# Attention between the second products: bundles of three and four slots by group of heads, instead of bundles of three across groups

## The chip, the cores and the metric

The kernel runs on one core of a Trainium2 chip. The metric is the device time of one execution in microseconds (us). An execution is also recorded by the hardware profiler; its span, its engines' busy times and its waits are what the readings below rest on.

## The reference

For q, k and v of shape (8, 12, 448, 64), that is 8 batches, 12 heads, 448 positions and 64 per head, the reference computes an attention with a squared relu, and then a layer norm with a feed-forward block on the 768 values of each position:

```python
scores = scale * np.matmul(q, k.transpose(0, 1, 3, 2))
attn = np.maximum(scores, 0.0) ** 2 / S
attn_out = np.matmul(attn, v)
x = attn_out.transpose(0, 2, 1, 3).reshape(B, S, H * D)
xn = (x - mu) / np.sqrt(var + 1e-06) * g_ln
out = x + np.maximum(xn @ w_ch1, 0.0) @ w_ch2      # w_ch1: 768 x 3072, w_ch2: 3072 x 768
```

Inputs and output are float32; the kernel multiplies in bfloat16 and sums in float32.

## The kernel before, in words

The kernel writes out the order of its work by hand: each engine executes its instructions in the order in which the Python code issues them. What one engine must wait for on another is left to semaphores.

Batches are taken in four pairs. For a pair, the positions of both batches (896, which are 7 blocks of 128 rows, `NT`) pass the feed-forward block together. Its first product (`ffn1`, L585, and for the later pairs also `ffn1_pair`, L663) gives hT. Its second product (`ffn2`, L627) is cut into units: 7 blocks, 2 halves of the 768 columns, 4 parts each, 56 units for a pair, and a unit is 6 matmuls into a PSUM tile `o_ps` (L634). After the fourth part of a half, VectorE evicts o_ps (`finish`, L645) and SP's queue stores the rows. `o_ps` comes from the pool ps_mm, which has two tiles.

While TensorE does the second products of one pair, it also does the attention of the next pair (`attention`, L522). There are three such stages in the kernel. The 12 heads of a batch are taken in 3 groups of four, so a pair of batches has 6 groups (`lo` to `hi`), and the keys of a group are cut into J = 7 slots. One slot is `scores(n, (i,), FULL)` (L327): four matmuls of 64 rows by 64 columns by 448 that use the four quarters of the array (L335), into a tile sc_ps of the pool ps_sc; ScalarE's relu (L346) takes it from PSUM into a tile attn_sb; VectorE squares that in place (L348). When all seven slots of a group are done, `values(n, FULL)` (L354) multiplies them with v: 28 matmuls (L365) into a tile av_ps, also of ps_sc; VectorE scales it into xT (L372) and makes xc of it (L388); GpSimd adds it to a running sum of the chunks (`chunks_summed`, L392). After the third group of a batch these sums are put on TensorE with a matrix of ones, and VectorE takes the mean out of xc (`centre`, L410).

ps_sc has three tiles, used in turn (`bufs=3`, L91): a slot, a product with v and the centring sum of an even batch each take the next one and wait until what last used it has been read. attn_sb has nine tiles.

`attention` returns a list of units, and `interleave` (L13) spreads them evenly between the units of the second product: after each of those it issues as many attention units as are due. So a list with fewer units leaves more second-product units between two of them. An attention unit is a *bundle* of slots, with a product with v in it where one is due:

```python
def item(n, i):
    scores(n, (i,), FULL)
    if i == J - 1 and n + 3 < len(groups):
        transposed(n + 3)

def product(n):
    values(n, FULL)
    load(n + 4, "v")
```

After a group's last slot, `transposed(n + 3)` issues the loads of k and q on GpSimd's queue and three transposing DMAs on SP's queue (L282, L287, L288) for a later group. The list ends with the product of the last group and with the second batch's `centre`.

Before, the 42 slots of a stage are cut into 14 bundles of three, across the bounds of groups. The product of group n - 1 stands behind the last of slots 1 and 2 of group n that is among the first two of a bundle: behind slot 2 as the first of its bundle (groups 1 and 4), behind slot 2 as the second of its bundle (groups 2 and 5), or behind slot 1 as the second (group 3). The first batch's `centre` is placed two bundles behind the bundle with its last product.

Of the kernel before, what the change touches and what calls it, by code (L numbers as in the profile page):

```python
# [28 lines left out]
def kernel(  # L29
# [32 lines left out]
    J = S // HP  # L62
# [55 lines left out]
    def load(n, names):  # L118
        if n >= len(groups):
            return  # L120
        b, m = groups[n]
        for name in names:
            if b == 1 and name != "v":
                o = (2 * m + "qk".index(name)) * 2 * S
                t = hold[:, o:o + 2 * S].rearrange("p (r s) -> p r s", r=2)
            elif name == "q":
                t = qbuf[m][:, D:D + 2 * S].rearrange("p (r s) -> p r s", r=2)
            else:
                t = io.tile([P, 2, S], bf16, tag=name, name=name + "_sb", bufs=4 if name == "v" else 3)
            nc.gpsimd.dma_start(t, srcs[name][b][:, m:NP:G, :])  # L130
            qkv[name, b, m] = t
# [27 lines left out]
    for queue, name, lo, hi in ((nc.sync, "q", 0, FEW), (nc.scalar, "k", 0, FEW),  # L159
                                (nc.sync, "k", FEW, J), (nc.scalar, "q", FEW, J)):  # L160
        s = slice(lo * D, hi * D)
# [165 lines left out]
    def scores(n, slots, blk):  # L327
        g, w = st[groups[n]], blk[1] * HP
        ps = ps_sc.tile([P, 2, 512], fp32, tag="sc", name="sc_ps")
        for o, i in enumerate(slots):  # L330
            for r in range(2):
                rows = slice(r * HP, (r + 1) * HP)
                for hh in range(2):
                    cols = slice(hh * HP, (hh + 1) * HP)
                    nc.tensor.matmul(  # L335
                        ps[cols, r, o * w:(o + 1) * w], g["k"](i)[rows, cols],
                        g["q"](i, r)[rows, blk[0]:sum(blk), cols], start=True, stop=True)
        if groups[n][0]:
            a = apool.tile([P, 2, 512], bf16, tag="attn", name="attn_sb")
        else:  # L340
            o = n_early[0] % 12 * 1024
            a = early[:, o:o + 1024].rearrange("p (r s) -> p r s", r=2)
            n_early[0] += 1
        since[0] = 0
        a = a[:, :, :len(slots) * w]
        nc.scalar.activation(a, ps[:, :, :len(slots) * w], ACTF.Relu)  # L346
        if blk == FULL:
            nc.vector.tensor_mul(a, a, a)  # L348
        else:
            later.append((n, a))  # L350
        for o, i in enumerate(slots):
            g["attn"].append(a[:, :, o * w:(o + 1) * w])

    def values(n, blk):  # L354
        squares_now(n)
        b, m = groups[n]
        v_sb, g, w = qkv["v", b, m], st[groups[n]], blk[1] * HP
        ps = ps_sc.tile([P, 2, 512], fp32, tag="sc", name="av_ps")
        for j in range(J):
            for hh in range(2):  # L360
                rows = slice(hh * HP, (hh + 1) * HP)
                for pr in range(2):
                    cols = slice(pr * HP, (pr + 1) * HP)
                    i, r = g["where"](pr, j)
                    nc.tensor.matmul(  # L365
                        ps[cols, hh, :w], v_sb[rows, pr, j * D:(j + 1) * D],
                        g["attn"][i][rows, r, :], start=(j == 0), stop=(j == J - 1))
        if b // 2 not in xT:
            xT[b // 2] = xpool.tile([P, K1, S2], bf16, tag="xT", name="xT_sb")
        if b not in xc:  # L370
            xc[b] = xcpool.tile([P, K1, S], bf16, tag="xc", name="xc_sb")
        nc.vector.tensor_scalar_mul(  # L372
            xT[b // 2][:, 2 * m:2 * m + 2, of(blk, b)], ps[:, :, :w], score_scale)
        if (b, blk) != FIRST:
            scaled(b, m, blk)
        g["attn"] = []
        since[0] = 9
        if blk == FULL:
            chunks_summed(b, m)
# [30 lines left out]
    def centre(b, blk):  # L410
        w = blk[1] * HP
        straight = (b, blk) == FIRST or blk == FULL and b % 2
        if straight:
            ps = ps_mm.tile([P, 512], fp32, tag="mm", name="sum_ps")[:, :w]
        else:
            ps = ps_sc.tile([P, 2, 512], fp32, tag="sc", name="sum_ps")[:, 0, :w]
        rows = [xT[b // 2][:, c, of(blk, b)] for c in range(K1)]
        if blk == FULL:
            rows = [part[b][:, i] for i in range(2)] + (rows[4:] if b % 2 else [])
        for i, r in enumerate(rows):  # L420
            nc.tensor.matmul(ps, ones, r, start=(i == 0), stop=(i == len(rows) - 1))  # L421
        total = ps
        if not straight:
            total = spool.tile([P, S], fp32, tag="total", name="total_sb", bufs=1)[:, :w]
            nc.scalar.copy(total, ps)
        for c in range(K1):
            nc.vector.scalar_tensor_tensor(
                xc[b][:, c, of(blk)], total, g_mean[:, c:c + 1], xc[b][:, c, of(blk)],
                op0=ALU.mult, op1=ALU.add)
# [3 lines left out]
    def transposed(n):  # L433

        if groups[n][0] < by_dma:
            transposes(*groups[n])
            return


        if n > by_dma * G:  # L440
            load(n + 2, "kq")
        keys_dma(n)
        queries_dma(n)

    def attention_block(b, blk):


        lo, hi, first = b * G, b * G + G, blk[0] == 0
        units = [lambda: transposed(lo)] if first else []

        def unit(n, part):
            squares_now()
            for i in range(4 * part, min(4 * part + 4, J), 2):
                scores(n, tuple(range(i, min(i + 2, J))), blk)
            if b == 1 and not first and part and n == hi - 1:
                transposed(hi)
            if part and n > lo:
                values(n - 1, blk)
                if not first:
                    load(n + 3, "v")  # L460
        for n in range(lo, hi):
            units.append(lambda n=n: unit(n, 0))
            if first and n + 1 < hi:
                units.append(lambda n=n: transposed(n + 1))
            units.append(lambda n=n: unit(n, 1))

        def last():
            values(hi - 1, blk)
            if b == 1 and not first:
                load(hi + 3, "v")  # L470
        units.append(last)
        units.append(lambda: centre(b, blk))
        return units
# [48 lines left out]
    def attention(bs):  # L522

        lo, hi = bs[0] * G, (bs[-1] + 1) * G
        seq = [(n, i) for n in range(lo, hi) for i in range(J)]  # L530
# [10 lines that stand above are left out]
        def bundle(items, at):  # L541
            for o, it in enumerate(items):
                item(*it)
                if o == at:
                    product(it[0] - 1)
        units, due = [], [[], []]
        for s in range(0, len(seq), 3):
            items = seq[s:s + 3]
            at = max((o for o, (n, i) in enumerate(items[:2]) if n > lo and i in (1, 2)), default=-1)
            units.append(lambda items=items, at=at: bundle(items, at))  # L550
            n = items[at][0] - 1
            due.append([groups[n][0]] if at >= 0 and groups[n][1] == G - 1 else [])
            units += [lambda b=b: centre(b, FULL) for b in due.pop(0)]
        units.append(lambda: product(hi - 1))
        units.append(lambda: centre(bs[-1], FULL))
        return units
# [428 lines left out]
    def ffn1_units(b, blk=FULL):  # L985
        if blk == FULL:
            return [lambda ni=ni: ffn1(b, ni, blk, b % 2 == 0) for ni in range(K2)]
        return [lambda: ffn1_head(b, blk)] + [lambda ni=ni: ffn1(b, ni, blk) for ni in range(3, K2)]

    def late_rows(n):  # L990

        last = [n // 2 - 1, n - 1]
        return [ki for ki in range(n) if ki not in last] + last
# [31 lines left out]
    units, side = ffn1_units(0, BLK[0][0]), attention_block(0, BLK[0][1])  # L1025
    units, late = units[:-4], units[-4:]
# [13 lines left out]
    units = ffn1_units(0, BLK[0][1])  # L1040
# [9 lines left out]
    for pair in range(pairs - 1):  # L1050
        units = ffn2_units(pair)
        if pair:
# [12 lines left out]
            units = units[2:]  # L1065
# [15 lines left out]
    def between(n):  # L1081
        for _ in range(4):
            gps.pop(0)()
        if n > 1 and side:
# [7 lines left out]
    units = [lambda half=half, part=part: ffn2(pair, 3, half, part, rows=late_rows(K2))  # L1092
             for half in range(2) for part in range(4)]
# [47 lines left out]
```

## Time and profile before

| what | value |
|---|---|
| median of 3 runs | 526.93 us (526.73 to 527.14) |
| the profiled execution's own time | 527.49 us |
| its span | 525.7 us |
| TensorE (PE) busy | 516.9 us, 98% of the span |
| VectorE (DVE) busy | 388.5 us, 74% |
| ScalarE (ACT) busy | 284.1 us, 54% |
| GpSimd (POOL) busy | 197.3 us, 38% |
| mean granted clock of TensorE | 1.00 |

The span runs from the first to the last instruction that the profiler recorded. In lines of the trace, PE is TensorE's matmuls and PEld its weight loads, which overlap; L335 is line 335 of the kernel; "x12" is a count, "128x896 bf16<-128x896 f32" the shapes written and read, and "64\*64" the part of the array that a matmul uses. What stands in brackets at the end of a line is how long the engine had been idle before it and whose instruction ended that idle time. In a list of waits the numbers are total us, how many times, and the longest.

### The profile page before, as it was taken

How to read it: one execution, taken by the hardware profiler on the slowest of the kernel's cores; microseconds unless marked ns; L12 is line 12 of the kernel's file. 1: busy time of each engine (PE TensorE's matmuls, PEld its weight loads, DVE VectorE, ACT ScalarE, POOL GpSimd, SP SyncE). 2: the span in 40 equal slices, each digit the busy share in tenths (PEclk: the TensorE clock that was granted, in tenths of full speed). 3: DMA queues.
4: the chain of work that ended last, by engine and by line, in shares of the span. 5: the costliest groups of instructions: out<-in, count | busy, mean ns of one | idle time of the engine just before them, and what ended most of it. 6: DMA issues, size and time to landing. Idle time of an engine off the chain costs nothing.

```text
span 525.7 us, 11571 instructions
## 1 busy us (share of the span) xinstructions
PE 516.9 (98%) x4612; PEld 305.5 (58%) x4612; DVE 388.5 (74%) x727; ACT 284.1 (54%) x478; POOL 197.3 (38%) x246
## 2 busy tenths in 40 slices
PE   8899999999999999999999999999999999999996
PEld 6678778755555555555555555555555554555663
DVE  5775654278898788758889779856989856886773
ACT  6966775465545266746646256647555435761110
POOL 7335102114624376002343727300330319991331
PEclk9999999999999999999999999999999999999999
DMA  9999999999988930216999885614651147421123
GB/s 196 206 206 207 211 192 164 172 159 139 171 137 153 185 68 0 36 31 102 169 170 179 134 206 172 157 36 62 131 104 46 46 111 185 116 88 31 38 54 91
DMA packets 121224, 66.50 MB, mean 126 GB/s; under 512 B 79698, under 2 KB 119890, under 8 KB 121170
## 3 DMA queue, kind: packets, MB, share of 16 engines
q1 hardware_dynamic: 92178, 37.05, 36.2%
q0 software_dynamic: 26976, 25.50, 33.0%
q10 hardware_dynamic: 2016, 3.21, 1.7%
q8 instruction: 36, 0.59, 0.5%
q14 instruction: 18, 0.15, 0.1%
HBM read 56.82 MB, written 15.93 MB: 138 GB/s over the span
## 4 chain that ended last, share of the span: by engine, by line
PE 93%; DMA 3%; POOL 2%; ACT 1%; DVE 1%; issue 0%; ACTq 0%; DVEq 0%; POOLq 0%
PE o_ps L634 34%; PE m_ps L752 21%; PE h_ps L596 15%; PE m_ps L885 8%; PE sc_ps L335 7%; PE av_ps L365 6%; DMA w<-in_moe_w_ch_dram 2%; PE h_ps L618 1%; DMA w_soon<-kept 1%; PE sum_ps L421 1%; ACT early L346 1%; PE tr_ps L220 1%; POOL v_sb L130 0%; POOL w L148 0%; POOL k_sb L130 0%
## 5 line engine op out<-in xcount | busy, mean ns | idle before, releaser
L634 PE MATMUL o_ps<-w,hT_sb 128*128 128x384 bf16 x1056 | 181.6, 326 | 0.0
L346 ACT ACTIVATE attn_sb<-sc_ps 128x896 bf16<-128x896 f32 (+4 forms) x150 | 126.4, 902 | 82.3 <-PE sc_ps L335 69.5
L634 PEld LDWEIGHTS <-hT_sb 128*128 128x128 bf16 x1056 | 99.6, 98 | 78.1 <-issue 15.2
L348 DVE TENSOR_TENSOR attn_sb<-attn_sb 128x896 bf16<-128x896 bf16 x126 | 81.6, 662 | 31.5 <-ACT attn_sb L346 26.9
L756 ACT ACTIVATE hT_sb<-m_ps 128x448 bf16<-128x448 f32 x120 | 65.2, 544 | 37.7 <-PE m_ps L752 35.7
L596 PE MATMUL h_ps<-xc_sb,w 128*128 128x192 bf16 (+2 forms) x648 | 82.2, 280 | 0.7 <-DMA w<-in_moe_w_ch_dram 0.3
L596 PEld LDWEIGHTS <-w 128*128 128x128 bf16 x648 | 58.1, 98 | 20.9 <-issue 3.1
L604 ACT ACTIVATE hT_sb<-h_ps 128x192 bf16<-128x192 f32 (+2 forms) x93 | 37.7, 406 | 56.8 <-PE h_ps L596 56.3
L400 POOL TENSOR_TENSOR part_sb<-xT_sb 128x448 f32<-128x448 bf16 x6 | 6.6, 1103 | 104.6 <-DVE xT_sb L372 84.9
L403 POOL TENSOR_TENSOR part_sb<-part_sb,xT_sb 128x448 f32<-128x448 f32 x18 | 23.3, 1295 | 55.6 <-DVE xT_sb L372 54.9
L846 POOL TENSOR_TENSOR w_sum_t<-w 128x384 bf16<-128x384 bf16 x48 | 41.8, 910 | 0.0
L752 PE MATMUL m_ps<-x_sum,w 128*128 128x448 bf16 x180 | 38.9, 352 | 0.0
L752 PE MATMUL m_ps<-xc_sb,w_sum 128*128 128x448 bf16 x168 | 36.4, 352 | 0.0
L572 DVE BATCH_NORM_STATS2 stats<-xtok_sb 128x6 f32<-128x384 bf16 x56 | 28.3, 546 | 10.7 <-DMA xtok_sb<-xT_sb 10.7
L335 PE MATMUL sc_ps<-qT_sb,kT_sb 64*64 64x448 bf16 x504 | 35.0, 358 | 0.0
L372 DVE TENSOR_SCALAR xT_sb<-av_ps 128x896 bf16<-128x896 f32 (+2 forms) x30 | 27.0, 901 | 7.8 <-PE av_ps L365 7.7
L365 PE MATMUL av_ps<-attn_sb,v_sb 64*64 64x448 bf16 (+2 forms) x672 | 32.3, 327 | 0.0
L752 PEld LDWEIGHTS <-w_sum 128*128 128x128 bf16 x210 | 20.5, 98 | 19.3 <-issue 0.3
L645 DVE SCALAR_TENSOR_TENSOR o_sb<-o_ps,rstd_sb,xtok_sb 128x384 f32<-128x384 f32 x44 | 26.6, 604 | 4.4 <-PE o_ps L634 4.4
L365 PEld LDWEIGHTS <-v_sb 64*64 64x64 bf16 x840 | 22.7, 107 | 11.8 <-issue 1.6
L388 DVE TENSOR_SCALAR xc_sb<-xT_sb,g_sb 128x448 bf16<-128x448 bf16 (+2 forms) x54 | 26.6, 541 | 1.0
L752 PEld LDWEIGHTS <-w 128*128 128x128 bf16 x180 | 17.6, 98 | 16.4
(144 smaller groups left out, 652.2 us busy)
## 6 DMA issues: line engine op xcount, KB each, us to landing
out_dram<-o_sb SPq DMA_DIRECT2D x90, 96.0 KB, 2.5
v_sb<-in_v_dram POOLq DMA_DIRECT2D x24, 224.0 KB, 5.3
w<-in_moe_w_ch_dram POOLq DMA_DIRECT2D x12, 384.0 KB, 13.9
w<-in_moe_w_ch_dram POOLq DMA_DIRECT2D x4, 1152.0 KB, 20.2
q_sb<-in_q_dram POOLq DMA_DIRECT2D x20, 224.0 KB, 6.6
k_sb<-in_k_dram POOLq DMA_DIRECT2D x20, 224.0 KB, 5.8
w_soon<-kept ACTq DMA_DIRECT2D x8, 288.0 KB, 3.5
w_late<-kept SPq DMA_DIRECT2D x10, 192.0 KB, 3.2
```

Of the source, the lines that this page charges most:

```text
L335: nc.tensor.matmul(ps[cols, r, o * w:(o + 1) * w], g["k"](i)[rows, cols], g["q"](i, r)[rows, blk[0]:sum(blk), cols], start=True, stop=True)
L346: nc.scalar.activation(a, ps[:, :, :len(slots) * w], ACTF.Relu)
L348: nc.vector.tensor_mul(a, a, a)
L365: nc.tensor.matmul(ps[cols, hh, :w], v_sb[rows, pr, j * D:(j + 1) * D], g["attn"][i][rows, r, :], start=(j == 0), stop=(j == J - 1))
L572: nc.vector.bn_stats(stats[:, n], xtok[pair][:, n * G:(n + 1) * G, t, :])
L596: nc.tensor.matmul(ps[:, :w], w1[:, c, ni * P:(ni + 1) * P], xc[b][:, c, of(blk)], start=(c == 0), stop=(c == K1 - 1))
L604: nc.scalar.activation(hT[pair][:, ni, o:o + w], ps[:, :w], ACTF.Relu)
L634: nc.tensor.matmul(ps[:, :DH], hT[pair][:, ki, t * P:(t + 1) * P], w2[:, ki, cols], start=(o == 0), stop=(o == K2 - 1))
L752: nc.tensor.matmul(ps, *at, start=(first and c == 0), stop=(c == KQ - 1), skip_group_check=not first)
L756: nc.scalar.activation(hT[pair][:, rows[n][row], half * S:(half + 1) * S], ps, ACTF.Relu)
L846: op(w2_sum[name][:, i:i + n], b[x][:, i:i + n], b[y][:, i:i + n])
L885: nc.tensor.matmul(ps, x[:, ki], y[:, ki], start=(first and ki == 0), stop=(ki == KH - 1), skip_group_check=not first)
```

## The change

The bundles are now cut by group: slots 0, 1, 2 in one bundle and slots 3, 4, 5, 6 in the next, 12 bundles a stage instead of 14. The product of group n - 1 always stands behind slot 0 of group n, as the second thing in the bundle of three. The first batch's `centre` follows one bundle behind the bundle with its last product instead of two. No instruction is added or removed: each engine executes the same ones in another order.

```diff
-        units, due = [], [[], []]
-        for s in range(0, len(seq), 3):
-            items = seq[s:s + 3]
-            at = max((o for o, (n, i) in enumerate(items[:2]) if n > lo and i in (1, 2)), default=-1)
+        units, due = [], [[]]
+        cuts = [n * J + i for n in range(hi - lo) for i in (0, 3)] + [len(seq)]
+        for s, e in zip(cuts, cuts[1:]):
+            items = seq[s:e]
+            at = max((o for o, (n, i) in enumerate(items[:1]) if n > lo and i == 0), default=-1)
             units.append(lambda items=items, at=at: bundle(items, at))
             n = items[at][0] - 1
             due.append([groups[n][0]] if at >= 0 and groups[n][1] == G - 1 else [])
             units += [lambda b=b: centre(b, FULL) for b in due.pop(0)]
```

Between two attention units of a stage there are now three or four second-product units (18 or 24 matmuls), as before, with four more often.

## The prediction

> **What bounds the kernel now.** I read the page first, for the engine that sets the end, then TensorE's own waits, then the order of work in one second-product stage, first TensorE alone and then all engines.
>
> The page:
>
> ```profile
> span 525.7 us, 11571 instructions
> PE 516.9 (98%) x4612; PEld 305.5 (58%) x4612; DVE 388.5 (74%) x727; ACT 284.1 (54%) x478; POOL 197.3 (38%) x246
> PE 93%; DMA 3%; POOL 2%; ACT 1%; DVE 1%; issue 0%; ACTq 0%; DVEq 0%; POOLq 0%
> ```
>
> TensorE is busy 98% of the span and carries 93% of the chain that ended last. So only what lengthens or shortens TensorE's own sequence moves the end. Its waits are short:
>
> ```profile
> PE idle_ps L206 <- DVE ones L99: 1.1, 1, 1.1
> PE av_ps L365 <- DMA v_sb<-in_v_dram: 0.7, 1, 0.7
> PE sc_ps L335 <- DVE early L223: 0.6, 2, 0.5
> ```
>
> These are the three longest of nine. None lies in the three stages that the change touches: by the busy times by stretch, TensorE is busy 75.20 of 75.20 us (99.8 to 175.0), 76.15 of 76.15 (222.9 to 299.0) and 76.20 of 76.20 (347.1 to 423.3). The stages run back to back:
>
> ```profile
> 111.92 3.10 PE L634 MATMUL o_ps<-w,hT_sb 128*128 128x384 bf16 x18
> 114.95 0.38 PE L335 MATMUL sc_ps<-qT_sb,kT_sb 64*64 64x448 bf16 x4
> 115.17 1.49 PE L365 MATMUL av_ps<-attn_sb,v_sb 64*64 64x448 bf16 x28
> 116.49 0.62 PE L335 MATMUL sc_ps<-qT_sb,kT_sb 64*64 64x448 bf16 x8
> 117.04 4.07 PE L634 MATMUL o_ps<-w,hT_sb 128*128 128x384 bf16 x24
> 121.04 0.76 PE L335 MATMUL sc_ps<-qT_sb,kT_sb 64*64 64x448 bf16 x12
> 121.74 3.10 PE L634 MATMUL o_ps<-w,hT_sb 128*128 128x384 bf16 x18
> 124.77 0.57 PE L335 MATMUL sc_ps<-qT_sb,kT_sb 64*64 64x448 bf16 x8
> 125.17 1.49 PE L365 MATMUL av_ps<-attn_sb,v_sb 64*64 64x448 bf16 x28
> ```
>
> The columns are start and duration. Four L335 matmuls are one slot, 28 L365 matmuls one product with v, six L634 matmuls one unit of the second product. Durations overlap at their ends, so I count from start to start. Last, the engines behind TensorE:
>
> ```profile
> 115.76 0.92 ACT L346 ACTIVATE attn_sb<-sc_ps 128x896 bf16<-128x896 f32 x1 [1.56 <-PE av_ps L365]
> 121.48 2.54 ACT L346 ACTIVATE attn_sb<-sc_ps 128x896 bf16<-128x896 f32 x3 [2.67 <-PE sc_ps L335]
> 122.43 0.63 DVE L348 TENSOR_TENSOR attn_sb<-attn_sb 128x896 bf16<-128x896 bf16 x1 [1.04 <-ACT attn_sb L346]
> 124.05 0.63 DVE L348 TENSOR_TENSOR attn_sb<-attn_sb 128x896 bf16<-128x896 bf16 x1 [0.18 <-ACT attn_sb L346]
> ```
>
> A slot takes TensorE 0.19 us; its relu takes ScalarE 0.92 us alone and 0.81 from one to the next (three in 2.54). The relu is what frees the slot's tile in ps_sc, and ps_sc has three tiles. A bundle of three slots just fits.
>
> **Fewer bundles: the part that is gained.** Six L634 matmuls take (4.00 - 3.03) = 0.97 us (24 from 117.04 to 121.04, 18 from 121.74 to 124.77), so 18 take 2.91. The 18 from 121.74 ended 3.03 later, so going to 64*64 costs 0.12. Three slots took 0.70 from 121.04 to 121.74, where three times 0.19 is 0.56, so going back costs 0.14. A bundle thus costs 0.26 beside its work. Two fewer in each of three stages: 6 x 0.26 = -1.6 us. The Trainium skill (TensorEngine Tiling, Key Properties) says that changing the tiling mode drains TensorE; by that rule alone the change would be this gain and nothing else, about 526.93 - 1.6 = 525.3 us. The trace agrees that a switch costs something, 0.12 and 0.14 us.
>
> **The fourth slot: the part that is lost.** The second bundle of each group holds slots 3 to 6: four ps_sc tiles in a row with no product between. The fourth goes into the first one's tile, and waits for its relu. From the bundle at 121.04: the first relu starts at 121.48, 0.44 after the first matmul, and lasts 0.92, so it ends 1.36 after. How long TensorE takes to go on is seen once in the lines above. In the bundle at 114.95 four tiles are asked for too (slot, product, slot, slot). Its first relu ended at 115.76 + 0.92 = 116.68; the last slot was ready at 116.49 + 0.19 = 116.68; its eight matmuls last 0.62, against 0.57 for the eight at 124.77. So TensorE goes on 0.05 after the relu's end, 1.41 after the bundle's start. Without a wait the fourth slot would start at 0.40 (two slots, 124.77 to 125.17) + 0.19 = 0.59. The wait is 0.82 us. Queued behind it on TensorE are the fourth slot and all second-product units after it, so nothing covers it. There are 6 such bundles in each of 3 stages: 18 x 0.82 = +14.8 us. Against the drain rule stands another of the Trainium skill (TensorEngine Tiling, PSUM Bottleneck): tiling speeds up TensorE but not the emptying of PSUM, which may then set the pace. The trace agrees, 0.19 us a slot against 0.81, and the sum goes by the measured rows.
>
> The bounds of this wait: if the tile came free at the relus' pitch of 0.81 and without the 0.05, it would be 0.44 + 0.81 - 0.59 = 0.66, or +11.9. If the first relu began as late as that at 115.76, 0.81 after its slot, it would be 1.19, or +21.4. I take 0.82, since the late one waited for a product that reads an attn_sb tile nine slots back, and the new order issues that product before every slot that needs it. ScalarE is also idle when a bundle begins (2.67 us before 121.48).
>
> **The product's place.** Where the product went behind the first slot of its bundle (groups 1 and 4, twice a stage), the third slot lost the 0.05 above: 6 x 0.05 = -0.3. In the new first bundles the first relu should start 0.44 after its slot and end at 1.36 + 0.05, while the third slot is reached at 0.22 + 1.32 + 0.19 = 1.73, so no wait. The product now follows the group's last slot sooner. In a bundle of four the relus start at 0.44, 1.25, 2.06 and 2.87, the last ends at 3.79, and its square at 4.45. TensorE leaves the bundle at 4 x 0.19 + 0.82 + 0.14 = 1.71, does 18 matmuls and a switch (3.03) and one slot (0.21), and begins the product at 4.95. It reads the last slot only in its sixth of seven steps, 0.95 later. Cover 1.4 us; if statistics (1.01 + 0.21) and an eviction (0.61) lay ahead on VectorE, 0.4 us would show in such a bundle.
>
> **Four squares on VectorE, and what is queued behind.** An o_ps eviction behind them starts at 4.5 instead of 3.7 us after the bundle and ends by 5.1, or 6.3 with statistics. The half that needs its bank starts after another 24 matmuls (3.88) and mostly a bundle with its product (2.0), at 1.71 + 0.97 + 5.9 = 8.6. Nothing.
>
> **The centring sum one bundle earlier.** It needs GpSimd's sums, done 6.7 us after the product's end (135.26):
>
> ```profile
> 137.51 2.67 POOL L403 TENSOR_TENSOR part_sb<-part_sb,xT_sb 128x448 f32<-128x448 f32 x2 [3.86 <-DVE xT_sb L372]
> 140.88 1.04 POOL L407 TENSOR_TENSOR two_sb<-part_sb,two_sb 128x448 bf16<-128x448 f32 x1
> 146.91 0.54 PE L421 MATMUL sum_ps<-two_sb,ones 128*128 128x448 bf16 x2
> ```
>
> Before, 5.0 us were to spare. In the new order the sum comes 0.51 (two slots) + 4.00 (24 matmuls) + 1.71 + 2.91 = 9.1 us after the product: 2.4 to spare. Were that cover gone by as much again, three sums would cost at most 7.
>
> **Loads, transposes, stores.** GpSimd's queue keeps its order, load(n+4, "v") behind the product included. On SP's queue the transposes of group n+3 stand among other output stores, which wait for evictions; they are needed two to three groups later, some 25 us. Nothing on TensorE.
>
> **Sum.** -1.6 + 14.8 - 0.3 = +12.9 us. The profiled execution took 527.49 us (span 525.7 and 1.8 around it), 0.56 above the median of 526.93. So 540.4 on its scale and **539.8 us** as a median.
>
> **Rivals.**
>
> *No wait at the fourth slot, and the switches win.* The time is 526.93 - 1.9 = 525.0. It decides where the wait is under 1.9 / 18 = 0.11 us a bundle, that is where TensorE may go on 0.59 + 0.11 = 0.70 us after the bundle's start. For it: TensorE shows no wait there today, and the queue has its work ready. Against it: the relu would have to take 0.70 - 0.44 - 0.05 = 0.21 us where the row has 0.92. This is also the case of a change that does not do what I read. Chance 0.04.
>
> *The first relu is late as well.* If ScalarE or VectorE falls behind in the closer order (VectorE is busy 58.8 of the first stage's 75.2 us), the wait goes towards 1.19 and the product and evictions wait too: +19.5, or 546.4. Against it: the waits themselves give VectorE 14.8 us more room. Chance 0.07.
>
> *The tile comes free early.* With 0.66 a bundle: +10.0, or 536.9. Chance 0.06.
>
> *The clock falls.* If after each wait the burst of 18 matmuls ran at half the granted clock, 18 x 2.91 = 52 us more, near 592. Against it: from 12 to 16 us TensorE was busy only 2.88 of 4.00 us and the granted clock in that window stayed 1.00. The Trainium skill (TensorE: Matmul & The Clock Gate, A second HAM failure mode) says that short idles between groups of matmuls, from cycling PSUM banks, can make the clock oscillate; no wait in this trace shows it. Chance 0.01.
>
> **Numbers.** The forecast, a wait near 0.82 in each of 18 bundles, has 0.82. The range 536.5 to 544.5 takes in the early tile, the forecast with half a microsecond a group lost on the late side (18 x 0.25 = 4.5), and leaves out the rest. It leaves out 0.12. Slower by over 0.2% (about what a measurement of this kernel can tell from no change) has 0.94: all cases but the one without a wait, less 0.02 for a wait so early (near 0.11 us) that it just cancels the gain, which is the same. Faster has 0.04.
>
> **What would show it.** Right: TensorE's list of waits gains an L335 line on ACT attn_sb L346 with 18 of about 0.8 us each, about 15 in all; the page's TensorE share falls to about 95%; a bundle of four lasts about 1.7 us to the next L634 matmul; each stage grows by about 4.3 us. The ScalarE wait on av_ps L365 (12.8 us in 6) goes away. Wrong: L335 shows no such wait or one under 0.3 us; or waits appear at L634 on VectorE, at L365 on the squares, or at L421 on GpSimd; or the granted clock falls under 1.00.

## The result: 2.6% slower, and the profile after

| | before | changed |
|---|---|---|
| median | 526.93 us (526.73 to 527.14, 5 runs) | 540.38 us (540.15 to 541.18, 5 runs) |
| profiled execution, its span | 527.49, 525.7 us | 540.83, 539.1 us |
| ratio | 1 | 1.0258 (95% interval 1.0243 to 1.0273) |

The change adds one line, so L634 is now L635; L335, L346, L365, L372 and L421 keep their numbers.

The page, its span, the engines and the chain that ended last:

```profile
span 539.1 us, 11569 instructions
PE 518.7 (96%) x4612; PEld 307.9 (57%) x4612; DVE 394.8 (73%) x727; ACT 283.3 (53%) x478; POOL 197.2 (37%) x246
PE 89%; DMA 5%; ACT 3%; POOL 1%; issue 1%; DVE 0%; POOLq 0%
```

Every engine in the second line has as many instructions as before, TensorE its 4612 matmuls; the two fewer in the first line are of none of them. TensorE's share falls from 98 to 96%, and ScalarE's share of the chain rises from 1 to 3%. TensorE's own waits, longest first, have a new first line:

```profile
PE sc_ps L335 <- ACT attn_sb L346: 11.5, 18, 0.6
```

There are 18 waits of scores for a relu, one for each bundle of four. The order of work on TensorE and ScalarE shows where they stand. These lines are from the first stage; columns are start and duration, and the bracket is the idle time before:

```profile
108.38 0.76 PE L335 MATMUL sc_ps<-qT_sb,kT_sb 64*64 64x448 bf16 x12
108.81 3.35 ACT L346 ACTIVATE attn_sb<-sc_ps 128x896 bf16<-128x896 f32 x4 [1.99 <-PE sc_ps L335]
109.78 0.38 PE L335 MATMUL sc_ps<-qT_sb,kT_sb 64*64 64x448 bf16 x4 [0.64 <-ACT attn_sb L346]
110.10 3.10 PE L635 MATMUL o_ps<-w,hT_sb 128*128 128x384 bf16 x18
113.12 0.38 PE L335 MATMUL sc_ps<-qT_sb,kT_sb 64*64 64x448 bf16 x4
...
113.56 0.92 ACT L346 ACTIVATE attn_sb<-sc_ps 128x896 bf16<-128x896 f32 x1 [1.40 <-PE sc_ps L335]
114.66 0.55 PE L335 MATMUL sc_ps<-qT_sb,kT_sb 64*64 64x448 bf16 x8
```

Three slots start at 108.38. ScalarE begins their relus at 108.81, idle until then. The fourth slot starts at 109.78, 1.40 us after the bundle's start, where 0.59 would do without a wait. So the wait is 0.81 us from start to start. The bracket says 0.64, because it counts from the modelled end of the matmul before, and that end lies about 0.17 us past the point where the next one could start. 18 x 0.81 = 14.6 us.

The first stage by stretch, for the changed kernel (the first number behind the bounds is its length, the second TensorE's busy time):

```profile
99.70:179.30 79.60, 75.76 (x680) 41.64 (x679) 60.40 (x106) 37.93 (x51) 28.79 (x34) 1.00 0.97 150
```

TensorE was idle 79.60 - 75.76 = 3.84 us, six times 0.64; before it was not idle at all in this stage. The other two stages read the same, 3.85 and 3.84 us. The granted clock (the number after the five engines) is 1.00 in all three. Counted in the trace from the first matmul of the unbroken second products of a stage to the first one of the next first product, the stages last 79.6, 77.7 and 77.7 us instead of 75.2, 73.3 and 73.3: 4.4 us longer each, 13.2 of the 13.4 us by which the span grew.

### The profile page after: what moved, and what is told of

It reads as the page before. It is cut to its first block, busy times and chain, and to the rows that moved or that the text cites. A ratio compares the mean times of both kernels' runs of the same rounds, so it can differ in the third digit from the quotient of the medians.

```text
span 539.1 us, 11569 instructions
## 1 busy us (share of the span) xinstructions
PE 518.7 (96%) x4612; PEld 307.9 (57%) x4612; DVE 394.8 (73%) x727; ACT 283.3 (53%) x478; POOL 197.2 (37%) x246
## 4 chain that ended last, share of the span: by engine, by line
PE 89%; DMA 5%; ACT 3%; POOL 1%; issue 1%; DVE 0%; POOLq 0%
PE o_ps L635 33%; PE m_ps L753 21%; PE h_ps L597 14%; PE m_ps L886 8%; PE sc_ps L335 6%; PE av_ps L365 6%; ACT attn_sb L346 3%; DMA w<-in_moe_w_ch_dram 3%; DMA v_sb<-in_v_dram 2%; PE h_ps L619 1%; DMA w_soon<-kept 1%; PE sum_ps L421 1%; PE tr_ps L220 1%; POOL k_sb L130 0%; POOL v_sb L130 0%
## 5 line engine op out<-in xcount | busy, mean ns | idle before, releaser
L635 PE MATMUL o_ps<-w,hT_sb 128*128 128x384 bf16 x1056 | 180.5, 327 | 0.0
L346 ACT ACTIVATE attn_sb<-sc_ps 128x896 bf16<-128x896 f32 (+4 forms) x150 | 125.9, 905 | 92.1 <-PE sc_ps L335 90.7
L635 PEld LDWEIGHTS <-hT_sb 128*128 128x128 bf16 x1056 | 100.1, 98 | 74.9 <-issue 11.1
L348 DVE TENSOR_TENSOR attn_sb<-attn_sb 128x896 bf16<-128x896 bf16 x126 | 86.6, 703 | 33.2 <-ACT attn_sb L346 30.3
L597 PEld LDWEIGHTS <-w 128*128 128x128 bf16 x648 | 58.1, 97 | 20.7 <-issue 2.9
L335 PE MATMUL sc_ps<-qT_sb,kT_sb 64*64 64x448 bf16 x504 | 36.9, 359 | 11.5 <-ACT attn_sb L346 11.5
L372 DVE TENSOR_SCALAR xT_sb<-av_ps 128x896 bf16<-128x896 f32 (+2 forms) x30 | 27.0, 901 | 9.2 <-PE av_ps L365 9.0
L335 PEld LDWEIGHTS <-kT_sb 64*64 64x64 bf16 x504 | 14.6, 105 | 32.5 <-issue 27.5
L365 PE MATMUL av_ps<-attn_sb,v_sb 64*64 64x448 bf16 (+2 forms) x672 | 32.3, 327 | 0.0
L753 PEld LDWEIGHTS <-w_sum 128*128 128x128 bf16 x210 | 20.5, 98 | 19.1
L365 PEld LDWEIGHTS <-v_sb 64*64 64x64 bf16 x840 | 22.8, 107 | 11.1 <-issue 1.6
```

What stands on the lines that cost most here:

```text
L335: nc.tensor.matmul(ps[cols, r, o * w:(o + 1) * w], g["k"](i)[rows, cols], g["q"](i, r)[rows, blk[0]:sum(blk), cols], start=True, stop=True)
L365: nc.tensor.matmul(ps[cols, hh, :w], v_sb[rows, pr, j * D:(j + 1) * D], g["attn"][i][rows, r, :], start=(j == 0), stop=(j == J - 1))
L597: nc.tensor.matmul(ps[:, :w], w1[:, c, ni * P:(ni + 1) * P], xc[b][:, c, of(blk)], start=(c == 0), stop=(c == K1 - 1))
L635: nc.tensor.matmul(ps[:, :DH], hT[pair][:, ki, t * P:(t + 1) * P], w2[:, ki, cols], start=(o == 0), stop=(o == K2 - 1))
L753: nc.tensor.matmul(ps, *at, start=(first and c == 0), stop=(c == KQ - 1), skip_group_check=not first)
```

## The experiments

The theory is that the fourth slot's wait for a tile of ps_sc is the whole loss, that two fewer bundles a stage are the whole gain, and that nothing else matters. Rivals are the product's new place with the earlier centring sum, and a backlog on ScalarE or VectorE from four slots in a row, whatever tile they free. The edits are against the changed kernel.

| kernel | median, us | before on the same chip | ratio (95% interval) | expected, us |
|---|---|---|---|---|
| 3, 2, 2 slots | 531.35 | 526.97 | 1.0097 (1.0065 to 1.0129) | 529.7 |
| 4, 3 slots, product behind slot 0 | 546.98 | 526.97 | 1.0377 (1.0360 to 1.0394) | 544.6 |
| 4, 3 slots, product behind slot 1 | 532.80 | 526.97 | 1.0114 (1.0099 to 1.0129) | 532.2 |
| first relu in two halves | 549.41 | 526.97 | 1.0436 (1.0401 to 1.0470) | 533.7 to 536.4 |
| first relu of one half only | 533.64 | 526.86 | 1.0128 (1.0111 to 1.0145) | 533.5 |
| 3, 2, 2 slots, centring sum later | 529.75 | 526.86 | 1.0051 (1.0036 to 1.0066) | 529.7 |
| 2, 2, 2, 1 slots | 534.35 | 526.86 | 1.0140 (1.0125 to 1.0155) | 534.4 |
| 13 bundles | 533.75 | 526.86 | 1.0128 (1.0113 to 1.0143) | 525.9 to 529.6 |
| four slots in three tiles | 525.60 | 527.21 | 0.9972 (0.9961 to 0.9983) | 525.2 |

**No bundle of four: 3, 2 and 2 slots.**

```diff
-        cuts = [n * J + i for n in range(hi - lo) for i in (0, 3)] + [len(seq)]
+        cuts = [n * J + i for n in range(hi - lo) for i in (0, 3, 5)] + [len(seq)]
```

> The changed kernel with slots 3 to 6 cut once more: bundles of 3, 2 and 2 slots, 18 a stage. The product stays behind slot 0 and the first batch's centre one bundle behind its last product. Theory (the fourth slot waits for the relu that frees its tile in ps_sc): no TensorE wait on ScalarE is left, and what remains is the price of bundles: 4 more than before in each of 3 stages, 12 x 0.26 = +3.1, less 0.3, so 526.9 + 2.8 = 529.7 us. Rival (the product behind slot 0 and the earlier centring sum cost the time): both are kept and the time stays near 540, with six more switches a stage above it, 543 to 545.

531.35 us: the loss is gone but for 4.4 us, with the product still behind slot 0 and the centring sum still one bundle behind. So neither place is the cause. No L335 wait on attn_sb is left. The time is 1.6 over the theory's, and TensorE's waits name it:

```profile
PE sum_ps L421 <- POOL two_sb L407: 1.0, 3, 0.5
```

With shorter bundles the centring sum, one bundle behind the last product, comes 6.0 us after that product's end (136.61 to 142.58), before GpSimd's sums (done 6.7 after). In the changed kernel this cover holds: the product ends at 137.18, the sums are done at 143.48 and used at 146.31, 2.8 us later.

**The same with the centring sum later.**

```diff
-        units, due = [], [[]]
+        units, due = [], [[], []]
```

with the cuts at 0, 3 and 5.

> The bundles of 3, 2 and 2 slots with the first batch's centring sum two bundles behind its last product instead of one. In the run with one bundle, TensorE waited for GpSimd's two_sb three times, about 0.6 us each from start to start. Theory: this wait goes and 18 bundles a stage cost 12 x 0.26 - 0.3 = +2.8 over the kernel before: 529.7 us, 1.6 under the run with one bundle. Rival (a bundle costs more than 0.26): stays at 531.3.

529.75 us, as expected. The wait for two_sb is gone, and that closes the miss of the run before.

**The price of a bundle: 2, 2, 2 and 1 slots.**

```diff
-        units, due = [], [[]]
-        cuts = [n * J + i for n in range(hi - lo) for i in (0, 3)] + [len(seq)]
+        units, due = [], [[], [], []]
+        cuts = [n * J + i for n in range(hi - lo) for i in (0, 2, 4, 6)] + [len(seq)]
```

> Bundles of 2, 2, 2 and 1 slots, 24 a stage, product behind slot 0, centring sum three bundles behind its last product. Theory (a bundle costs 0.26 us in switches and nothing waits): 30 bundles more than the kernel before in all, 30 x 0.26 - 0.3 = +7.5, so 534.4 us, with no TensorE wait on ScalarE. Rival (short bundles also cost waits, as the squares of slot 6 come just before the product): 537 or more, with a wait at L365.

534.35 us. The three stages, from bounds as above, grew by 2.65, 2.17 and 2.17 us for 30 more bundles. The first has a TensorE wait that the theory did not have, the longer of the two in this line (the other lies ahead of the stages):

```profile
PE sc_ps L335 <- DVE xT_sb L372: 0.5, 2, 0.3
```

It ends at 153.57, just after VectorE has read a product's tile, late, behind the centring, an eviction and a square. With 0.17 added as above it costs about 0.46, near the 0.48 between the first stage and the others. So bundles alone cost 3 x 2.17 = 6.5 us, and with the 0.3 of the old wait added back (6.5 + 0.3) / 30 = 0.23 us each. The prediction had 0.26, and the 0.24 in the expectation of the run with three tiles below still has that wait in it. That the time met the forecast is in part luck: a wait that was not forecast stood against a cheaper bundle.

**The wait follows the tile: 4 and 3 slots, product behind slot 0.**

```diff
-        cuts = [n * J + i for n in range(hi - lo) for i in (0, 3)] + [len(seq)]
+        cuts = [n * J + i for n in range(hi - lo) for i in (0, 4)] + [len(seq)]
```

> The changed kernel with the cut after slot 3: slot 0, product, slots 1, 2, 3 in one bundle, slots 4, 5, 6 in the next; 12 bundles a stage. Theory (the ring of three tiles): slot 3 now goes into the product's tile, which VectorE frees when it has scaled it into xT. In the changed kernel that ends 3.01 us after the bundle's start; slot 3 is reached at 0.22 + 1.32 + 0.38 = 1.92, so it waits 1.14 us in 15 bundles, and 0.82 in the 3 first groups, which have no product: 17.1 + 2.5 - 1.9 = +17.7, so 544.6 us, and the wait is named after VectorE, L372, not after the relu. Rival (four relus in a row hold ScalarE up, whatever tile they free): the product now spreads the four relus over 2 us, so the wait becomes smaller than in the changed kernel and the time is under 536.

546.98 us. TensorE's waits:

```profile
PE sc_ps L335 <- DVE xT_sb L372: 16.1, 16, 1.7
PE sc_ps L335 <- ACT attn_sb L346: 2.1, 3, 0.8
```

VectorE and TensorE in the first such bundle, which began at 113.09:

```profile
115.02 1.08 DVE L372 TENSOR_SCALAR xT_sb<-av_ps 128x896 bf16<-128x896 f32 x1
116.15 0.38 PE L335 MATMUL sc_ps<-qT_sb,kT_sb 64*64 64x448 bf16 x4 [0.98 <-DVE xT_sb L372]
```

The same number of bundles of four, but the wait now ends 3.06 us after the bundle's start (116.15), 0.05 after VectorE has read the product's tile (115.02 + 1.08 = 116.10), as computed. Only the three first groups, without a product, still wait for ScalarE. A wait for a backlog of ScalarE would have shrunk. The time is 2.4 us over the sum. Of the 16 waits for VectorE 15 are in these bundles; six of them are longer than the 0.98 shown, up to 1.68, where VectorE began the scaling later, and two of the three for ScalarE are longer than 0.64. That is 1.4 us in all; the other 1.0 stays open.

**The wait shrinks with the tile's age: 4 and 3 slots, product behind slot 1.**

```diff
-            at = max((o for o, (n, i) in enumerate(items[:1]) if n > lo and i == 0), default=-1)
+            at = max((o for o, (n, i) in enumerate(items[:2]) if n > lo and i == 1), default=-1)
```

with the cuts at 0 and 4.

> As the kernel with the cut after slot 3, but the product stands behind slot 1: slots 0, 1, product, slots 2, 3, then slots 4, 5, 6. Theory (ring of three): slot 2 takes slot 0's tile (reached at 0.40 + 1.32 = 1.72, free at 1.41), slot 3 takes slot 1's, whose relu ends at 0.44 + 0.81 + 0.92 = 2.17; slot 3 is reached at 1.91, so it waits 2.22 - 1.91 = 0.31 in 15 bundles and 0.82 in the 3 first groups: 4.7 + 2.5 - 1.9 = +5.3, so 532.2 us. Rival (bundles of four slots are what costs, by ScalarE's four relus): as many bundles of four as in the changed kernel, so near 540.

532.80 us, 0.6 over the theory and 7 under the rival. Slots 2 and 3 behind the product:

```profile
114.97 0.87 PE L335 MATMUL sc_ps<-qT_sb,kT_sb 64*64 64x448 bf16 x8
```

Eight such matmuls behind a product without a wait last 0.55 (114.66 in the changed kernel), these 0.87: 0.32 us, where 0.31 was computed.

**A shorter read of the first tile, first try: the relu in two halves.**

```diff
-        nc.scalar.activation(a, ps[:, :, :len(slots) * w], ACTF.Relu)
+        if blk == FULL and slots == (3,):
+            nc.scalar.activation(a[:, 0], ps[:, 0, :w], ACTF.Relu)
+            nc.vector.tensor_scalar_max(a[:, 1], ps[:, 1, :w], 0.0)
+        else:
+            nc.scalar.activation(a, ps[:, :, :len(slots) * w], ACTF.Relu)
```

> The changed kernel, with the relu of slot 3 (first of each bundle of four) in two halves: ScalarE takes one, VectorE the other. Theory (the wait is the time to the end of that one relu): ScalarE's half takes about 0.54 us (the 128x448 relus of L757), so it ends at 0.98; VectorE's about 0.6 if it is free. The wait falls from 0.82 to between 0.45 and 0.6, and the time from 540.4 by 18 x 0.22 to 18 x 0.37, to 533.7 to 536.4 us. Rival (product's place, centring sum or VectorE's load cost the time): no gain, or more than 540.4, since VectorE has 18 x 0.6 us more to do.

549.41 us, slower than the changed kernel: by its number this is what the rival said, and the theory's number failed. The trace tells why. The halves did not run beside each other (L348 is VectorE's half here):

```profile
108.43 0.76 PE L335 MATMUL sc_ps<-qT_sb,kT_sb 64*64 64x448 bf16 x12
...
108.87 0.54 ACT L347 ACTIVATE attn_sb<-sc_ps 128x448 bf16<-128x448 f32 x1 [1.98 <-PE sc_ps L335]
...
109.44 0.62 DVE L348 TENSOR_SCALAR attn_sb<-sc_ps 128x448 bf16<-128x448 f32 x1 [0.29 <-ACT attn_sb L347]
...
110.12 0.38 PE L335 MATMUL sc_ps<-qT_sb,kT_sb 64*64 64x448 bf16 x4 [0.93 <-DVE attn_sb L348]
```

VectorE was idle 0.29 us and waited for ScalarE's half. That the program orders the two because both halves belong to one tile is our reading, not shown. So the tile's last reader ended at 109.44 + 0.62 = 110.06, later than the whole relu would have (0.44 + 0.92 = 1.36 after 108.43, at 109.79), and the fourth slot followed 0.06 after. In 15 of the 18 bundles the wait was 0.93 like this one; in three it was about 1.7, as VectorE was still at an eviction, so its load had a part, as the rival said. The 18 waits add up to 19.1 us in the list instead of 11.5, and a slow stretch, told of at the end, adds 1.7: together 9.3 us, beside the 9.2 by which the three stages outgrew the changed kernel's. The size was missed because the halves were taken to be free of each other and VectorE to be free; that the slot goes on with the end of the tile's last reader held.

**A shorter read, second try: one reader of half the columns.**

```diff
+        if blk == FULL and slots == (3,):
+            nc.scalar.activation(a[:, 0], ps[:, 0, :w], ACTF.Relu)
+            nc.vector.tensor_mul(a[:, 1], a[:, 0], a[:, 0])
+            nc.vector.tensor_mul(a[:, 0], a[:, 0], a[:, 0])
...
```

The other slots keep their relu and square.

> The changed kernel, with the first slot of each bundle of four (slot 3) relu'd by ScalarE for one half of its columns only, before one square for each half from it: the other half of that slot's scores is left out, so its tile has one short reader, which takes about 0.54 us. Theory (the wait is the time to the end of the tile's last reader): 0.44 + 0.54 + 0.05 = 1.03 after the bundle's start instead of 1.41, so TensorE's wait falls by 0.38 in 18 bundles and the time from 540.4 to 533.5 us. Rival (product's place or the centring sum): unchanged, 540.

533.64 us, 6.7 less than the changed kernel; 18 x 0.38 = 6.8 was computed. The bundle that starts at 108.38 here goes on at 109.41, 1.03 after, as computed:

```profile
109.41 0.38 PE L335 MATMUL sc_ps<-qT_sb,kT_sb 64*64 64x448 bf16 x4 [0.27 <-ACT attn_sb L347]
```

**The wait taken away, the bundles kept: four slots in three tiles.**

```diff
+        if blk == FULL and slots == (J - 1,):
+            ps = shared[0]
+        else:
+            ps = shared[0] = ps_sc.tile([P, 2, 512], fp32, tag="sc", name="sc_ps")
...
+        if blk == FULL and slots == (J - 2,):
+            shared[1] = a
+        elif blk == FULL and slots == (J - 1,):
+            for x in (shared[1], a):
+                nc.scalar.activation(x, ps[:, :, :w], ACTF.Relu)
+                nc.vector.tensor_mul(x, x, x)
...
```

> The changed kernel with all its bundles, products and centring sums in place, but slot 6's matmuls write into slot 5's tile, so that a bundle of four needs three tiles; slot 5's scores are left out (both relus read slot 6's). The same number of matmuls, relus and squares. Theory (the fourth tile is the whole loss, and 12 bundles instead of 14 the whole gain; a bundle cost 0.24 us in the runs with 18 and 24): no TensorE wait on ScalarE, 526.9 - 6 x 0.24 - 0.3 = 525.2 us. Rival (four slots in a row cost in themselves, through ScalarE's or VectorE's queue, or the product's place does): above 527.

525.60 us, 0.3% faster than the kernel before, with an interval wholly below 1. It leaves out slot 5's scores, so it shows a cause and is no kernel to use. A bundle of four on TensorE, and the second products behind it:

```profile
108.29 0.95 PE L340 MATMUL sc_ps<-qT_sb,kT_sb 64*64 64x448 bf16 x16
109.17 3.10 PE L649 MATMUL o_ps<-w,hT_sb 128*128 128x384 bf16 x18
```

It takes 0.88 us to the next second product instead of the 1.72 of the changed kernel. The stages are 0.61, 0.60 and 0.60 us shorter than before, 1.81 in all, where 6 x 0.24 + 0.3 = 1.74 was computed (1.68 with 0.23). Same bundles, same products' places, same centring sum, four relus in a row: with the fourth tile's wait alone gone, each stage is (4.41 + 0.61) = 5.02 us shorter than in the changed kernel, 0.84 us for each of six waits.

**A version that might have kept the gain: 13 bundles.**

```diff
+        cuts = [0, 3, 5] + [n * J + i for n in range(1, hi - lo) for i in (0, 4)] + [len(seq)]
...
+        if blk == FULL and slots == (0,) and n % (2 * G):
+            nc.vector.tensor_scalar_max(a, ps[:, :, :w], 0.0)
...
```

with the product behind slot 1.

> 13 bundles a stage: 3, 2 and 2 slots in the first group, then slots 0, 1, product, 2, 3 and slots 4, 5, 6 in each other group; in these the relu of slot 0 is done by VectorE (128x896 from PSUM, about 1.08 us as L372) and that of slot 1 by ScalarE. Theory (ring of three): slot 2 is reached at 1.72 and slot 0's tile is free at 0.44 + 1.08 + 0.05 = 1.57 if VectorE is free; slot 3 is reached at 1.91, and slot 1's relu, now first on ScalarE, ends near 1.6. Nothing waits, and 3 bundles fewer give -0.8, and -0.3 for the old wait at the third slot: 525.9 us, 0.2% under the kernel before. If VectorE is still busy with statistics or squares when such a bundle starts, slot 2 waits by what is left: half a microsecond in half of 15 bundles would make it 529.6. Rival (bundles of four slots cost by themselves): 536 or more.

533.75 us, above both bounds. TensorE waited for VectorE's relu six times, up to 1.6 us. VectorE and TensorE in one of these bundles, which starts at 135.22:

```profile
135.04 1.01 DVE L576 BATCH_NORM_STATS2 stats<-xtok_sb 128x6 f32<-128x384 bf16 x2
...
136.21 0.60 DVE L649 SCALAR_TENSOR_TENSOR o_sb<-o_ps,rstd_sb,xtok_sb 128x384 f32<-128x384 f32 x1
136.73 1.08 DVE L347 TENSOR_SCALAR attn_sb<-sc_ps 128x896 bf16<-128x896 f32 x1
...
137.86 0.38 PE L335 MATMUL sc_ps<-qT_sb,kT_sb 64*64 64x448 bf16 x4 [0.56 <-DVE attn_sb L347]
```

VectorE executes in order; statistics and an eviction came first, and the relu began 1.5 us after the bundle's start instead of 0.44. The half microsecond allowed for in half of the bundles was too little.

## Why the prediction was right, step by step

*The fourth slot* carried the result, and its size held: 0.82 us predicted; 0.81 measured in the bundle, 0.84 by the run that takes the wait away. The start at 0.44, the relu's 0.92 and the 0.05 to go on all came out as read from the trace of before. That the wait belongs to the tile and not to four slots as such was only argued in the prediction; three runs show it. The wait moved to VectorE with the tile, fell to 0.32 with an older tile, and went away with three tiles in use.

*The gain of fewer bundles* is real, 0.23 us each instead of 0.26, so -1.4 instead of -1.6 us. It never showed in the changed kernel, since it is worth a tenth of the waits. The rule that changing the tiling mode drains TensorE (the Trainium skill, TensorEngine Tiling, Key Properties) agrees with a cost at the switch, here 0.23 us for the two of a bundle. The section PSUM Bottleneck of the same page of the Trainium skill says that emptying PSUM may become the bottleneck. A relu of 0.92 us against a slot of 0.19 agrees, but that pace alone cost nothing: in the run with three tiles in use the same four relus followed one another, and TensorE did not wait. What decided was the number of tiles.

*The product's place* cost nothing: eight matmuls behind it last 0.55 us and no longer 0.62 (six times 0.07, so -0.4 instead of -0.3), the first relu starts 0.44 after its slot (113.12 to 113.56), and ScalarE's old wait for av_ps (12.8 us in 6) is gone from the list of waits. *The centring sum* kept 2.8 us of cover (2.4 predicted), and one run showed what it costs without: about 0.5 us a stage. *Squares, evictions, loads and stores*: no TensorE wait on any of them appears in the three stages of the changed kernel, whose idle time is the 18 waits alone.

The rivals: the one without a wait is what the run with three tiles in use shows, 525.6 us beside the 525.0 given for it. A late first relu, an early tile and a slower clock did not appear in the changed kernel. What was off is how the wait would show: the list of waits has 11.5 us, not 15, for the reason given with the trace above, and TensorE's share is 96%, not 95%, for the same reason. The sum, +12.9 us, stands against a measured 13.45. With the measured terms it is 18 x 0.84 - 1.4 - 0.4 = 13.3, beside 13.2 for the three stages, though the 0.84 comes from the same stages. The misses of the two smaller terms, 0.2 and 0.1 us, partly cancel.

## What to carry to other kernels

Where, as here, a burst of work asks a pool for one tile more than the pool has, it waits for the first tile's whole reading: count from the burst's start to the end of the last reader, take off when the burst reaches that tile, and multiply by the bursts. Compare that with the switch saved before merging bursts; here 0.82 us lost stood against two switches, 0.23 us, for each bundle saved, and the wait came three times as often. Two ways round it failed here: handing the first tile to another engine, which in some of the bundles was not free at that moment, and splitting a tile between two engines, which did not read it at once.

## What the runs showed of the hardware beyond that

In the run with the relu in two halves TensorE once waited 1.74 us in the middle of dense matmuls, and 0.7 us after the wait's end the granted clock fell. TensorE alone:

```profile
302.38 0.38 PE L335 MATMUL sc_ps<-qT_sb,kT_sb 64*64 64x448 bf16 x4 [1.74 <-DVE attn_sb L348]
302.70 5.76 PE L639 MATMUL o_ps<-w,hT_sb 128*128 128x384 bf16 x24
```

The stretch behind the wait, with the granted clock as the number after the five engines:

```profile
302.70:306.40 3.70, 3.70 (x17) 1.83 (x14) 2.13 (x4) 0.92 (x1) 2.15 (x4) 0.55 0.78 121
```

24 second-product matmuls took 5.7 us instead of 4.0. In steps of a tenth of a microsecond the granted clock stood at 0.50 from 303.1 to 306.5, 3.4 us, and was back at 1.00 behind that. Behind four other waits of 1.62 to 1.74 us, in this run and two others, the second products kept their usual pace, and so they did behind all 18 waits of 0.64 us in the changed kernel. Another execution of the same kernel had a mean granted clock of 1.000, where such a fall makes it 0.997, and took 548.39 us beside the 549.48 of the one shown. The Trainium skill (TensorE: Matmul & The Clock Gate, A second HAM failure mode) says that short idles between groups of matmuls can make the clock oscillate. Here there is one fall and no oscillation, behind an idle time well under the 3.4 us that the same page of the Trainium skill (Part 1: The HAM clock gate) gives for one idle window. That the wait caused the fall is not shown, and what decides between such a wait and the next was not tried.
